# Weaving the first mixing visit into the second half of the phases, and plain products for two visits (long convolution with wave-MLP, one core)

## Chip, cores and metric

The kernel runs on one core of a Trainium2 chip. The metric is the device time of one execution in microseconds (us), lower is better. T, S and the other marks on the time axis are read from the profiled execution of each kernel and count from the start of its span.

## The reference

```python
B, S, D = 8, 5696, 128
y  = irfft(rfft(x, 2*S) * rfft(h, 2*S))[:, :S]     # long convolution, per batch and channel
theta = y @ w_theta                                 # phases
zr, zi = y * cos(theta), y * sin(theta)
m  = einsum('ts,bsd->btd', w_tok_r, zr) + einsum('ts,bsd->btd', w_tok_i, zi)   # token mixing
u  = y + m
out = u + maximum(u @ w_ch, 0)
```

The kernel first does the convolution, then the phases of the first 2816 tokens in two halves (batches 0 to 3, then 4 to 7; 22 steps of 128 tokens each), then the token mixing, which takes the rest, some 1585 of 2175 us, other work running behind it. Mixing goes in "visits" of two pairs of output tiles; its operand b (z of these tokens, eleven blocks of 128 x 4096 bf16, each with a left half from batches 0 to 3 and a right half from batches 4 to 7) stays in SBUF for a whole pass of 22 visits. Most visits are by Strassen's scheme, seven products in place of eight, for which VectorE makes sums of the parts of b; the first visit was by plain products while those sums were made.

## The kernel before, where the change touches it

```python
# last group of the convolution: y (yt) to HBM
    if then is not None:
        then(yt)                       # ya of the second phase half, SBUF to SBUF, on SyncE
    for e in range(2):
        nc.sync.dma_start(yt_hbm[...], yt[64 * e:64 * e + 64]...)
# ... cut ...
def phase_step(ti, hh):                # one of 22 steps of a half
    yT = st[hh][:, :, ti * P:(ti + 1) * P]
    # 4 transposes (tpz), 10 theta matmuls, then
    def copy():
        nc.vector.tensor_copy(y_ap, tpz)
        nc.sync.dma_start(y2_hbm[ti]..., y_ap...)
    phases_b(ti, y_ap, 4 * hh, 4, yT, ..., copy=copy)
# phases_b: three activations (ScalarE), zr and zi into zz (VectorE), then per 64 rows
    nc.sync.dma_start(z_hbm[:, p_, j, i, :, cols].rearrange("z t n -> t z n"), zz[rows])
# ... cut ...
def load_b(p, j, pool):                # a block of b back from HBM
    t_ = pool.tile([P, 7 * 1024], BF16, tag=f"b{j}", name=f"b{j}")
    for z in range(2):
        eng = nc.scalar if p or j >= NE else nc.sync
        eng.dma_start(t_[:, z * 2048:(z + 1) * 2048], z_hbm[z, p, j]...)

for step in steps0:                    # first half
    step()
for n, ti in enumerate(tile_order):    # second half, b blocks loaded behind it
    phase_step(ti, 1)
    if n % 4 == 3:
        while len(bts_of[0]) < min(n // 2, NE):
            load_b(0, len(bts_of[0]), bpe)
# ... cut: mixing ...
classic = tt == 0                      # visit 0 plain, all others Strassen
if classic:
    for n in range(4):
        for j in range(nj):
            # 4 products of 512 columns per block and n
    for j in range(nj):
        sums_apart(bts[j0 + s0 + j]); sums_in_place(bts[j0 + s0 + j])     # VectorE
    for c, z, m_ in (...):
        nc.vector.tensor_tensor(c, z, ms[m_], op=add)                     # y added by VectorE
```

## Time and profile before

2178.68 us (median of 3 runs, 2177.13 to 2178.82); the span of the profiled run is 2175.5 us. The stages, from the table of busy time in chosen windows:

| stage | from, us | to, us | TensorE busy, us | clock | DMA share |
|---|---|---|---|---|---|
| end of convolution, first phase half | 400.0 | 463.5 | 48.6 | 0.95 | 0.67 |
| second phase half | 463.5 | 549.4 | 34.6 | 0.71 | 0.98 |
| visit 0 | 549.4 | 590.8 | 41.0 | 0.94 | 0.94 |
| from visit 1 to the end | 590.8 | 2175.5 | about 15 us of waits | 1.00 (to 1286.4) | 0.93 (to 1286.4) |

Read it so: after 590.8 us TensorE is full and its clock is full, so there nothing can be gained but by less work. "Clock" is the share of TensorE's full clock that was granted, "DMA share" the mean busy share of the core's 16 DMA engines as the profile counts it, which can pass 1. Names in the profile: yt is y as the convolution leaves it; ya is y of one phase half as the steps read it, and two copies ya<-yt fill the last part of the second half's; tpz and theta_ps are a step's transposes and phases on TensorE; y_ap is the copy of y that is stored, zz the z of one step; ring is, in the changed kernel, the place in SBUF of the early weights and of block 0 of b. Two marks: **S**, the moment at which the steps of the second half can go on because ya has landed (465.8 us), and **T**, the moment at which visit 0 is done and visit 1 starts (590.8 us). The span is S + (T - S) + rest = 465.8 + 125.0 + 1584.7.

### The profile page before, as it was taken

The numbers are of one execution on the slowest core, as the hardware profiler recorded it, in microseconds if no ns is written. First come the engines' busy times: TensorE is split into PE (matmuls) and PEld (weight loads), VectorE is DVE, ScalarE is ACT, GpSimd is POOL, SyncE is SP. The second block draws the span as 40 slices with busy tenths as digits, with TensorE's granted clock in tenths as the row PEclk, the third lists the DMA queues.
The fourth block names the chain that finished last, engine by engine and source line by source line (L and its number), as shares of the span: only waits on it lengthen the run. The fifth ranks groups of instructions, "written<-read, shape, count | busy, mean of one in ns | idle before, by whom it ended". The sixth has DMA issues, their size and how long they took to land.

```text
span 2175.5 us, 41105 instructions
## 1 busy us (share of the span) xinstructions
PE 1998.2 (92%) x15545; PEld 1125.1 (52%) x15723; DVE 1619.4 (74%) x2920; ACT 670.6 (31%) x984; POOL 857.1 (39%) x1572
## 2 busy tenths in 40 slices
PE   4788898763899999999999999899999999999998
PEld 4787888652344444444444444344444444444444
DVE  7767767767778888888877667667777777776867
ACT  5877877574132333333210000001111111111111
POOL 5301010002344645445466544354545453535350
PEclk8788889987899999999999999999999999999999
DMA  7356463579988989899999869687878787879794
GB/s 146 89 125 163 128 162 118 172 185 275 236 156 175 182 169 168 167 179 176 176 169 162 138 115 291 106 133 137 148 132 152 132 151 130 152 131 153 126 158 91
DMA packets 409382, 340.38 MB, mean 156 GB/s; under 512 B 83303, under 2 KB 363751, under 8 KB 408071
## 3 DMA queue, kind: packets, MB, share of 16 engines
q0 software_dynamic: 221312, 143.00, 48.7%
q1 hardware_dynamic: 183552, 179.93, 28.5%
q10 hardware_dynamic: 4320, 14.81, 1.8%
q8 instruction: 123, 2.02, 0.4%
q14 instruction: 75, 0.61, 0.1%
HBM read 381.83 MB, written 97.93 MB: 221 GB/s over the span
## 4 chain that ended last, share of the span: by engine, by line
PE 65%; DMA 5%; DVE 4%; issue 2%; ACT 2%; POOL 1%; SPq 1%; DVEq 0%; ACTq 0%; POOLq 0%
PE m L910 59%; DMA b<-z_hbm 3%; PE m L878 2%; DMA z_hbm<-zz 2%; DVE c L917 1%; PE v L680 1%; PE utp L673 1%; PE m L914 1%; DVE wt L591 1%; PE m L833 1%; POOL wb L582 1%; PE m L831 1%; ACT mag L404 0%; ACT red L405 0%; PE theta_ps L382 0%
## 5 line engine op out<-in xcount | busy, mean ns | idle before, releaser
L582 POOL DMA_DIRECT2D wb<-in_moe_w_tok_i_dram x720 | 387.9, 547 | 679.3 <-DVE wt L591 602.6
L591 DVE STREAM_TRANSPOSE wt<-wb 128x384 f32<-128x384 f32 (+2 forms) x720 | 360.2, 524 | 117.1 <-PE m L910 71.2
L582 POOL DMA_DIRECT2D wb<-in_moe_w_tok_r_dram x720 | 386.6, 548 | 146.2 <-DVE wt L591 107.0
L910 PE MATMUL m<-b,wt 128*128 128x512 bf16 x1803 | 425.7, 381 | 7.1 <-DVE wt L591 2.4
L910 PEld LDWEIGHTS <-wt 128*128 128x128 bf16 x1848 | 181.3, 98 | 225.0 <-issue 5.7
L917 DVE TENSOR_TENSOR c<-c,m 128x512 f32<-128x512 f32 x420 | 271.0, 671 | 0.4 <-PE m L910 0.4
L675 ACT ACTIVATE uts<-utp 128x512 bf16<-128x512 bf16 (+1 forms) x90 | 53.2, 592 | 607.3 <-PE utp L673 607.3
L320 PE MATMUL ps<-r_u,u_t 128*128 128x128 f16 x1024 | 133.0, 228 | 14.9 <-DVE u_t L304 11.7
L321 PE MATMUL ps<-r_v,v_t 128*128 128x128 f16 x1024 | 131.7, 227 | 0.0
L670 ACT ACTIVATE ub<-c 128x512 bf16<-128x512 f32 (+1 forms) x90 | 56.3, 628 | 224.9 <-DVE c L846 139.7
L127 POOL DMA_DIRECT2D x<-in_x_dram x64 | 34.2, 541 | 201.3 <-PE ps L190 189.3
L320 PEld LDWEIGHTS <-u_t 128*128 128x128 f16 x1024 | 106.0, 103 | 13.6 <-DVE u_t L304 13.5
L321 PEld LDWEIGHTS <-v_t 128*128 128x128 f16 x1024 | 104.9, 103 | 5.2 <-issue 3.7
L304 DVE TENSOR_TENSOR u_t<-xs,hs 128x1024 f16<-128x1024 f16 x96 | 69.6, 725 | 41.9 <-ACT xs L302 31.5
L302 ACT ACTIVATE xs<-ps 128x1024 f16<-128x1024 f32 x96 | 95.3, 1017 | 17.6 <-DVE v_t L304 8.7
L878 PE MATMUL m<-b,wt 128*128 128x512 bf16 x344 | 79.3, 387 | 15.3 <-ACT red L405 14.5
L190 PE MATMUL ps<-f_t,x 89*128 89x180 f16 x512 | 84.5, 310 | 8.0 <-ACT xs L302 5.9
L208 PEld LDWEIGHTS <-w_t 64*128 64x128 f16 x3240 | 65.5, 106 | 38.1 <-issue 24.7
L580 POOL COPY wb<-b 128x2 bf16<-128x2 bf16 x4 | 0.5, 179 | 213.2 <-DMA z_hbm<-zz 213.2
L190 PEld LDWEIGHTS <-x 89*128 89x128 f16 x512 | 73.8, 237 | 10.1 <-issue 9.4
L384 ACT ACTIVATE red<-theta_ps,magic 128x512 f32<-128x512 f32 (+1 forms) x46 | 31.6, 687 | 140.8 <-PE theta_ps L382 107.4
L623 ACT ACTIVATE yb<-tpz 128x512 bf16<-128x512 bf16 (+1 forms) x46 | 27.4, 597 | 153.6 <-PE tpz L621 137.4
(2713 smaller groups left out, 3824.5 us busy)
## 6 DMA issues: line engine op xcount, KB each, us to landing
wb<-in_moe_w_tok_r_dram POOLq DMA_DIRECT2D x352, 96.0 KB, 4.5
wb<-in_moe_w_tok_i_dram POOLq DMA_DIRECT2D x352, 96.0 KB, 5.0
wb<-in_moe_w_tok_r_dram POOLq DMA_DIRECT2D x352, 80.0 KB, 4.2
wb<-in_moe_w_tok_i_dram POOLq DMA_DIRECT2D x352, 80.0 KB, 3.7
hs<-hf_hbm SPq DMA_DIRECT2D x192, 128.0 KB, 3.2
cp_hbm<-c SPq DMA_DIRECT2D x88, 256.0 KB, 2.3
c<-cp_hbm SPq DMA_DIRECT2D x88, 256.0 KB, 4.0
out_dram<-c SPq DMA_DIRECT2D x88, 256.0 KB, 4.2
```

Source lines behind the costliest of these rows:

```text
L190: nc.tensor.matmul(ps[:, i // 2, (i % 2) * 2 * K1:(i % 2 + 1) * 2 * K1], lhs(q + i), f1_t[:NB], start=True, stop=True)
L208: nc.tensor.matmul(ps[:, e, j * HD:(j + 1) * HD], w_t2[rows, c0 + j, N2 * (1 - ri):N2 * (3 - ri)], a_st["a"][rows, ri * K1 + c0 + j, :], s ...
L302: nc.scalar.activation(xs[:, :, :, :ck], ps, AF.Copy)
L304: nc.vector.tensor_tensor(uv[r][:, :, :, c0:c0 + ck], xs[:, :, :, :ck], hv[:, r:r + 1, :, :ck].to_broadcast([P, 2, HD, ck]), op=mult)
L320: nc.tensor.matmul(o, u_t[:, at:at + P], r_u, start=True, stop=False)
L321: nc.tensor.matmul(o, v_t[:, at:at + P], r_v, start=False, stop=True)
L582: nc.gpsimd.dma_start(wb[32 * i:32 * i + 32, :ng, :nj * 64], bass.AP(tensor=a.tensor, offset=a.offset + row0 * S + p * H + i * QR + j0 * 6 ...
L591: nc.vector.transpose(wt.rearrange("p j t r -> p (j t r)").bitcast(F32).rearrange("p (j g t) -> p g j t", j=TJ, g=4)[:, :ng, :nj], wb[:, : ...
L670: nc.scalar.activation(ub[:m].rearrange("p b d -> p (b d)"), c[:m], AF.Copy)
L878: nc.tensor.matmul(ms[n // 2 * 2 + h], a[n][:, j, :, r], bts[jj][n % 2 * 2 + h][:, r, :], start=(n % 2 == 0 and jj == 0 and r == 0), stop= ...
L910: nc.tensor.matmul(ms[q], a[q][:, j, :, r], bts[jj][q][:, r, :], start=(jj == 0 and r == 0), stop=(jj == NJ - 1 and r == 1 and q not in left))
L917: nc.vector.tensor_tensor(c, z, ms[q], op=op)
```

## The change

Its intent: TensorE idles through the second phase half, so do the products of visit 0 there, four after each step. For this, z of the right half goes from SBUF straight into b for nine of eleven blocks, left halves are fetched ahead, the weights of visits 0 and 1 are fetched before the phases end, stores of y and part of z move from SyncE to GpSimd's queue, visit 1 becomes plain too so that VectorE's sums can be spread over more time, and y is added on TensorE by identity matmuls and evacuated by ScalarE.

```diff
@@ the last yt stores, the stores of y in the second half @@
-                    nc.sync.dma_start(yt_hbm[...], yt[...])
+                    (nc.gpsimd if then else nc.sync).dma_start(yt_hbm[...], yt[...])
-            nc.sync.dma_start(y2_hbm[ti]..., y_ap...)
+            (nc.gpsimd if hh else nc.sync).dma_start(y2_hbm[ti]..., y_ap...)
@@ z straight into b @@
+            if tags is None and j in home:
+                for r in range(2):
+                    (nc.gpsimd if e and r else nc.sync).dma_start(
+                        home[j][32 * i:32 * i + 32, :4096]...[:, :, q_, r], zz[e * 64 + r:e * 64 + 64:2])
+            elif tags is None:
+                nc.sync.dma_start(z_hbm[:, p_, j, q_, i].rearrange("z t n -> t z n"), zz[rows])
@@ weights early, in a ring where a table of the convolution was @@
+    def open_ring():
+        ring["all"] = keep.tile([P, K1 * 3 * N2], BF16, tag="keep", name="ring")
+        pump()
@@ left halves ahead @@
+    def load_b_half(j):
+        t_ = home_of[j] = tile_b(0, j, home_pool(j))
+        for z in range(2):
+            nc.gpsimd.dma_start(t_[:, z * 2048:z * 2048 + 1024], z_hbm[z, 0, j, 0]...)
+    for j in range(7):
+        load_b_half(j)
     for step in steps0:
         step()
@@ the weave: blocks 0 to 5 of visit 0 in four quarters, left column half first @@
+        if i == 1:
+            for q, (h, s) in enumerate(((0, 0), (0, 1), (1, 0), (1, 1))):
+                for n in range(4):
+                    for j in range(TJ):
+                        product((held, a)[s], s * TJ + j, j, n, (h,))
+                        if (n * TJ + j) % 2:
+                            next_steps(1)
@@ blocks 9 and 10 still through HBM, once the phases are done @@
+        for j in range(len(bts_of[0]), NJ):
+            load_b(0, j, bp)
@@ plain visit 1, y by identity matmuls @@
-            classic = tt == 0
+        classic = plain(p, tt)           # tt == 0 or (p == 0 and tt == 1)
+                        if n == 1:
+                            nc.tensor.matmul(ms[m_], ident_bf, z, start=False, stop=True)
+                        else:
+                            for b in range(4):
+                                nc.tensor.matmul(ms[m_][:, b * D:(b + 1) * D], z[:, b, :], ident_bf, ...)
+                        nc.scalar.activation(c, ms[m_], AF.Copy)
... (cut: the ring of weights, the spread of VectorE's sums, the order of background work)
```

## The prediction

> **What bounds the kernel now.** I read the page's busy table and slices first, then the busy time by stage, then the waits of TensorE in two windows, then the time order of single engines around the change of stage.
>
> ```profile
> PE   4788898763899999999999999899999999999998
> PEclk8788889987899999999999999999999999999999
> ```
>
> From slice 11 (598 us) on TensorE is full at full clock: that is the token mixing. Slices 8 to 10, counted from 0 (435 to 598 us), are the hole: there the second half of the phases runs (theta, sine, cosine, z for batches 4 to 7). The stages, from the table of busy time in chosen windows (us, then busy us and count of each engine, clock, DMA share, GB/s):
>
> ```profile
> 400.00:463.50 63.50, 48.57 (x690) 41.41 (x701) 47.79 (x76) 43.95 (x76) 0.00 (x0) 0.95 0.67 172
> 463.50:549.40 85.90, 34.58 (x304) 25.00 (x309) 57.77 (x106) 43.50 (x76) 19.11 (x39) 0.71 0.98 254
> 549.40:590.80 41.40, 41.02 (x188) 18.75 (x192) 30.17 (x53) 8.01 (x13) 11.61 (x22) 0.94 0.94 230
> 590.80:1286.40 695.60, 686.95 (x3408) 323.42 (x3476) 560.00 (x1092) 171.10 (x276) 360.71 (x664) 1.00 0.93 166
> ```
>
> Row 2, the second phase half, lasts 85.9 us with TensorE busy 34.6 (and that at a clock of 0.71) and no compute engine over 58; the DMA share is 0.98. Row 3 is the first mixing visit (plain products), row 4 the Strassen visits of pass 0. Who held TensorE up, in 463 to 591 us:
>
> ```profile
> PE ps L482 <- ACT red L405: 34.6, 16, 10.2
> PE m L878 <- ACT red L405: 14.5, 1, 14.5
> ```
>
> ScalarE is named, but it was itself starved, as its time order shows (idle before, then releaser):
>
> ```profile
> 531.35 0.60 ACT L404 ACTIVATE mag<-ps 128x512 f32<-128x512 f32 x1 [9.78 <-DVE y_ap L486]
> 548.16 0.60 ACT L404 ACTIVATE mag<-ps 128x512 f32<-128x512 f32 x1 [7.21 <-DVE y_ap L486]
> ```
>
> The copy into y_ap waits for a free y_ap, that is for the store of y to HBM, which sits in SyncE's queue behind stores of z and loads of b. So the stage is bound by transfers: z goes out to HBM and comes back as b, while weights are already being loaded. Where nothing blocks (480 to 493 us) a step takes 1.66 us, ScalarE's three activations. Mixing then begins cold:
>
> ```profile
> 549.38 0.59 PE L878 MATMUL m<-b,wt 128*128 128x512 bf16 x1 [14.51 <-ACT red L405]
> 590.84 1.46 PE L910 MATMUL m<-b,wt 128*128 128x512 bf16 x6
> 595.59 2.72 PE L910 MATMUL m<-b,wt 128*128 128x512 bf16 x6 [2.21 <-DVE c L893]
> ```
>
> After 590.8 TensorE waits for some 15 us in all up to the end, so what counts is when the visit after the first begins, plus the work that is left then.
>
> **What the Trainium skill says.** "TensorE: Matmul & The Clock Gate", section "Back-to-back issue gap": N/2.4 + 2.5 ns for a warm matmul of N columns, 216 ns at 512. The trace agrees: starts at 1286.65, 1286.86, 1287.08 us. The same page, "Why this matters for your kernels", wants no TensorE gaps over some 3 us lest the clock halve; here it fell to 0.71 on average in row 2, and the first matmul after the gap has 0.59 us instead of 0.38. "DMA: Bandwidth & Descriptors", "Issuing engines are not separate DMA queues": DMAs of all issuers run on the same 16 engines, so moving stores from SyncE to GpSimd saves issue time only. Row 2's 0.98 agrees. "PSUM — Partial Sum Buffer", "Engine vs sequencer instructions": matmuls start and complete in program order. So mixing woven between phase steps cannot slip past a blocked step; the 34.6 us above show such blocking.
>
> **The change part by part.** Let T be the time at which the second mixing visit starts. Before, T = 590.8.
>
> (a) Weaving. The first six of eleven j blocks of visit 0 (6 x 16 = 96 matmuls of 512 columns) go between the 22 phase steps: 96 x 0.216 = 20.7 us. A step on TensorE has 4 transposes and 8 theta matmuls of 128 columns and 2 of 512: 2560 columns, 12 x 0.056 + 2 x 0.216 = 1.1 us; 22 of them 24 us. Sum 45 us, or 2.0 us per step with its four products, more than ScalarE's 1.66. Start: the first step of this half ran at 463.5 and waited for ya until 465.8. I take 465, so these would end at 510 if only TensorE counted. The left halves need no second-half phases, so the first two of four quarters can start at once; the scratch banks of the phases are apart from the four accumulators.
>
> (b) Five more j blocks: 80 x 0.216 = 17.3 us, then 2 identity matmuls of 512 and 8 of 128, 0.9 us. Ideal T = 510 + 18 = 528. The accumulators are evacuated by ScalarE (4 x 0.6 us beside), so the wait of 2.2 us for DVE c goes.
>
> (c) Transfers in 465 to 528. z of the right half goes SBUF to SBUF, 22 x 256 KB = 5.8 MB, written once and not read back for nine of eleven blocks. y 22 x 128 KB = 2.9 MB. Blocks 9 and 10 still come from HBM, 2.1 MB. Left halves: nine of 0.5 MB; their places (and the ring's) come free one by one from 400 us on and their z is complete tile by tile, so I guess that five load before 463, where row 1 has a share of only 0.67, and 2 MB remain. Final yt and ya 2 MB. Together 14.8 MB on the queues that took 28.5% of the 2175 us for 180 MB, 3.45 us per MB: 51 us. Six weight loads of 0.38 MB on the queue with 48.7% for 143 MB, 7.4 us per MB: 17 us. Sum 68 us of 63 us of window. In stretches of 20 us the share reached 1.04 to 1.15 between 520 and 580 us, so it almost fits, but it comes in bursts: I add 9 us. T = 537. Before, the same stage also sent 8 MB of b back in.
>
> (d) Visit 1 plain, not Strassen: 176 instead of 154 matmuls, +22 x 0.216 = 4.8 us, plus 0.9 us of identities. Two background steps move from visit 0 to later, +0.9 us.
>
> (e) Operand sums: 11 x 5 of 0.6 us (0.68 busy) = 33 us of DVE, formerly all in visit 0, now spread up to visit 2. DVE in the rest of visit 0 and in visit 1: 48 sums 29 us, some 24 transposes 12 us, background 6 us, weight sums 3 us: 50 us of 57. Close; I allow 2 us of waits.
>
> (f) Removed after T: the wait and cold clock around 593 us, -3 us.
>
> Rest: before 2175.5 - 590.8 = 1584.7 us; after 1584.7 + 4.8 + 0.9 + 0.9 + 2 - 3 = 1590.3. Span 537 + 1590 = 2127; the times lie 2 to 3 us above the span (2178.7 to 2175.5): 2130 us, 2.2% less.
>
> **The rivals.** First, the weave flows: transfers and issue hide entirely, T = 528 and no DVE waits: 2119 us. For it: TensorE needs 2.0 us per step where ScalarE needs 1.66, and z no longer makes the round trip. Against it: the 68 us of transfers above. Second, the queues become the bound. GpSimd must issue per step a y store and part of z (about 1.0 us, from its 0.547 us per issue), plus 24 weight pieces and left halves (15 to 20 us): 37 to 42 us of 45, in order. One late landing there holds up the stores of y, four y_ap run out, and in-order TensorE stops the products too. SyncE has three z pieces per step; its z stores take 0.59 us to issue, 1.8 us per step at worst. If steps took 2.6 us, T = 550: 2143 us. Third, the early weights (2.4 MB from about 400 us, 17 us of DMA) delay ya for the first phase half, whose loads are issued at 400.5 and 404 us; a late ya stops TensorE in order. At most 5 us, partly absorbed since TensorE is busy only 48.6 of 63.5 us in row 1. Fourth, DVE becomes the bound in visit 1 (85% or more even by my count): +5 to 10 us. Fifth, the gain is hidden anyway: unlikely, since TensorE has no slack after 600 us, so an earlier start comes out nearly whole at the end.
>
> **Range and chances.** The limit for over 2% is 2135 us, 5 us above my sum. The queues and DVE could cost 10 to 15 us more, a smooth weave gives back 11. So 2112 to 2150 for 8 in 10; faster by over 2% 0.65, within 2% 0.33, slower 0.02.
>
> **What would show it.** Right: TensorE over 85% busy from 470 us on, with the clock near 1; the last phase step at about 515 us; the second visit starting at 528 to 546; z landing in b directly; the later visits at 33.5 us each as now. Wrong: TensorE waiting on ScalarE or VectorE during the weave with gaps of 5 us and more (queues or DMA, second rival); waits for ya before 430 us (third); TensorE waiting for wt or b sums in visits 1 and 2 (fourth); a start at 537 with an end that has not moved by as much, which would mean a new loss in the steady visits.

## The result, and the profile after

The changed kernel takes 2153.16 us (median of 4 runs, 2152.45 to 2157.64) against 2177.96 us (2177.13 to 2178.82) of the kernel before in the same rounds: a ratio of 0.989, with a 95% interval of 0.9873 to 0.9908. A ratio is the mean time of one kernel's runs over that of the other's runs of the same rounds, so it is not quite the ratio of the medians quoted. The result is correct. It is 1.1% faster, and 3 us above the predicted range of 2112 to 2150. The profiled run is the slowest of the four (span 2155.9 us), which matters for a few us below.

The two rows of the page that the prediction began with, busy tenths of TensorE and granted clock in 40 slices of 54 us, now of the changed kernel:

```profile
PE   3788889768999999999999997999999999999998
PEclk8699879999999999999999999999999999999999
```

The hole in slices 8 to 10, counted from 0 (6, 3, 8 before), has become 6, 8, 9, with the clock at 9 in place of 8, 7, 8: largely filled, but not its first third. The same stages as before, of the changed kernel (from:to and length in us, then busy us and count of TensorE, weight load, VectorE, ScalarE, GpSimd, then clock, DMA share, GB/s):

```profile
400.00:463.50 63.50, 48.12 (x732) 41.58 (x742) 51.18 (x83) 47.43 (x81) 15.21 (x28) 0.95 0.95 228
463.50:549.40 85.90, 63.42 (x448) 37.01 (x457) 53.52 (x100) 43.08 (x74) 46.12 (x84) 0.87 0.92 240
549.40:590.80 41.40, 40.11 (x184) 18.03 (x186) 26.78 (x48) 9.64 (x16) 13.97 (x27) 0.89 0.76 152
590.80:1286.40 695.60, 687.37 (x3409) 324.70 (x3477) 554.95 (x1084) 172.69 (x279) 357.45 (x658) 1.00 0.92 165
```

In the second row TensorE is busy 63.4 us where it was 34.6, in the time that half of the phases took before, but the DMA share is still 0.92: the weave runs in a stage that transfers fill. The first row's DMA share has gone from 0.67 to 0.95. The last row is as before. The same stretch cut where the changed kernel changes its pace:

```profile
470.85:490.00 19.15, 12.38 (x80) 7.74 (x83) 10.75 (x21) 9.83 (x17) 11.32 (x21) 0.77 1.01 341
490.00:520.00 30.00, 29.07 (x253) 18.21 (x256) 22.00 (x40) 22.57 (x40) 22.82 (x42) 1.00 0.98 230
520.00:533.40 13.40, 10.06 (x60) 5.61 (x60) 6.29 (x13) 7.91 (x14) 4.39 (x8) 0.75 0.74 189
533.40:562.40 29.00, 23.34 (x100) 10.03 (x100) 18.93 (x36) 1.82 (x4) 13.93 (x26) 0.82 0.87 188
562.40:602.20 39.80, 39.59 (x202) 18.88 (x205) 30.04 (x53) 12.81 (x22) 13.00 (x25) 1.00 0.81 153
```

Row 2 is the weave as it was meant: TensorE busy 29.07 of 30 us at full clock. Before it (row 1) and after it (row 3) it stalls at a reduced clock, and the tail of visit 0 (row 4) is slow too. Row 5 is the plain visit 1, full. S and T by TensorE's time order (start, length, then idle before and its releaser):

```profile
470.85 0.29 PE L561 MATMUL tpz<-ident_bf,ya 128*128 128x128 bf16 x1 [5.42 <-DMA ya<-yt]
561.84 0.61 PE L1002 MATMUL m<-ident_bf,yy 128*128 128x128 bf16 x8
```

S = 470.85 and T = 561.84 + 0.61 = 562.45 us. The rest after T is 2155.9 - 562.45 = 1593.5 us. The prediction had S = 465, T = 537 and a rest of 1590.3. So of the 29 us by which this profiled span passes the predicted 2127, 25 lie before T: 6 us in S and 20 us in T - S (91.6 in place of 72); the other 3 are in the rest. What TensorE waited for from 463 to 620 us (us in all, times, longest; the first four of seven lines):

```profile
PE tpz L561 <- DMA ya<-yt: 6.9, 2, 5.4
PE m L964 <- DMA b<-z_hbm: 5.8, 4, 3.4
PE tpz L561 <- DVE y_ap L569: 5.2, 2, 3.7
PE m L964 <- DMA b<-zz: 3.9, 2, 3.2
```

Before, 49 us of such waits stood against ScalarE and, behind it, the stores of y; now four kinds of waits share what is left, three for transfers and one for y_ap. A wait costs more than its own length, since matmuls after it run at the lower clock: in row 1 the waits and the clock of 0.77 took 19.15 us for 80 matmuls. GpSimd's queue in the same time (start, length, issues, idle before):

```profile
457.85 1.11 POOL L354 DMA_DIRECT2D yt_hbm<-yt  x2 [22.11 <-issue]
471.69 4.26 POOL L626 DMA_DIRECT2D b<-z_hbm  x8 [12.74 <-DMA z_hbm<-zz]
...
485.44 0.54 POOL L570 DMA_DIRECT2D y_hbm<-y_ap  x1
```

Only block 0's left half was loaded before S; the eight others go out from 471.69 us on, and the first store of y of this half stands behind them until 485.44. VectorE, too, was held up in this stretch:

```profile
479.50 0.69 DVE L417 TENSOR_TENSOR zz<-red,y_ap 128x512 bf16<-128x512 f32 x1 [4.63 <-DMA z_hbm<-zz]
```

It waited 4.63 us here, and 2.74 us more at 483.87, until stores of the first half's last z had landed and their zz was free. And the two ya copies, from issue to landing, before and after:

```profile
ya<-yt SPq DMA_DIRECT2D x2, 352.0 KB, 4.1
```
```profile
ya<-yt SPq DMA_DIRECT2D x2, 352.0 KB, 9.2
```

### The profile page after: what moved, and what is told of

It is laid out like the page before. It is cut to its first block, busy times and chain, and to the rows that moved or that the text cites. A ratio compares the mean times of both kernels' runs of the same rounds, so it can differ in the third digit from the quotient of the medians.

```text
span 2155.9 us, 41270 instructions
## 1 busy us (share of the span) xinstructions
PE 2000.3 (93%) x15586; PEld 1124.8 (52%) x15765; DVE 1599.6 (74%) x2884; ACT 674.7 (31%) x992; POOL 889.7 (41%) x1628
## 4 chain that ended last, share of the span: by engine, by line
PE 64%; DVE 3%; DMA 2%; issue 1%; ACT 0%; POOL 0%; DVEq 0%; ACTq 0%
PE m L1034 58%; PE m L964 2%; DMA b<-z_hbm 2%; DVE c L1041 1%; PE v L776 1%; PE utp L769 1%; PE m L1038 1%; DVE wt L689 1%; PE m L921 1%; PE m L919 1%; PE theta_ps L385 0%; PE tpz L717 0%; DMA yT<-yt_hbm 0%; DMA y_hbm<-ring 0%; POOL ring L493 0%
## 5 line engine op out<-in xcount | busy, mean ns | idle before, releaser
L493 POOL DMA_DIRECT2D ring<-in_moe_w_tok_i_dram x720 | 388.2, 547 | 686.2 <-DVE wt L689 612.1
L493 POOL DMA_DIRECT2D ring<-in_moe_w_tok_r_dram x720 | 386.8, 548 | 240.9 <-PE ps L211 103.5
L689 DVE STREAM_TRANSPOSE wt<-ring 128x384 f32<-128x384 f32 (+2 forms) x720 | 357.9, 522 | 116.3 <-PE m L1034 69.9
L1034 PEld LDWEIGHTS <-wt 128*128 128x128 bf16 x1804 | 176.6, 98 | 215.7 <-DVE wt L689 3.2
L1041 DVE TENSOR_TENSOR c<-c,m 128x512 f32<-128x512 f32 x412 | 265.1, 669 | 0.4 <-PE m L1034 0.4
L771 ACT ACTIVATE ring<-utp 128x512 bf16<-128x512 bf16 (+1 forms) x86 | 50.9, 592 | 608.6 <-PE utp L769 608.6
L307 DVE TENSOR_TENSOR u_t<-xs,hs 128x1024 f16<-128x1024 f16 x96 | 69.8, 727 | 42.8 <-ACT xs L305 23.8
L964 PEld LDWEIGHTS <-wt 128*128 128x128 bf16 x528 | 51.4, 101 | 69.8 <-issue 17.0
L719 ACT ACTIVATE ring<-tpz 128x512 bf16<-128x512 bf16 (+1 forms) x46 | 27.4, 597 | 137.2 <-PE tpz L717 115.8
```

The lines of the kernel that those rows point to most:

```text
L307: nc.vector.tensor_tensor(uv[r][:, :, :, c0:c0 + ck], xs[:, :, :, :ck], hv[:, r:r + 1, :, :ck].to_broadcast([P, 2, HD, ck]), op=mult)
L493: nc.gpsimd.dma_start(wb[32 * i:32 * i + 32, :ng, :nj * 64], bass.AP(tensor=a.tensor, offset=a.offset + row0 * S + p * H + i * QR + j0 * 6 ...
L689: nc.vector.transpose(wt.rearrange("p j t r -> p (j t r)").bitcast(F32).rearrange("p (j g t) -> p g j t", j=TJ, g=4)[:, :ng, :nj], wb[:, : ...
L964: nc.tensor.matmul(ms[n // 2 * 2 + h], a[n][:, j, :, r], bts_of[p][jj][n % 2 * 2 + h][:, r, :], start=(n % 2 == 0 and jj == 0 and r == 0), ...
L1034: nc.tensor.matmul(ms[q], a[q][:, j, :, r], bts[jj][q][:, r, :], start=(jj == 0 and r == 0), stop=(jj == NJ - 1 and r == 1 and q not in left))
L1041: nc.vector.tensor_tensor(c, z, ms[q], op=op)
```

## The experiments

The question was which of these made the 25 us between the predicted and the measured T. Theories at the start: A, separate losses (a late ya, left halves that wait for their place, the tail of blocks 9 and 10, SyncE's many issues), each worth its waits; B, the stage is bound by the 16 DMA engines, so that taking one wait away brings up another. A third question arose, what the weave itself had brought. Kernels were made, on five chips, each with runs of the kernel before on its own chip. All numbers in one table ("full DMA" is DMA share times T - S, that is, how long all 16 engines would need if their packets took the same time; it falls by itself when the stage gets shorter, so it is a description and no proof of a bound):

| run | median us (range) | ratio to before | S | T | T - S | rest | full DMA |
|---|---|---|---|---|---|---|---|
| before | 2178.0 (2177.1 to 2178.8) | 1 | 465.8 | 590.8 | 125.0 | 1584.7 | 121 |
| change | 2153.2 (2152.5 to 2157.6) | 0.9890 | 470.9 | 562.4 | 91.6 | 1593.5 | 84 |
| e11_after_again | 2152.3 (2146.3 to 2157.1) | 0.9881 | 471.8 | 560.3 | 88.5 | 1589.3 | 84 |
| e1_yt_sync | 2151.1 (2149.2 to 2155.0) | 0.9883 | 468.5 | 561.9 | 93.4 | 1591.3 | 90 |
| e2_places | 2148.6 (2144.6 to 2152.7) | 0.9869 | 469.3 | 553.0 | 83.7 | 1589.8 | 79 |
| e3_half_issue (wrong) | 2152.1 (2147.2 to 2153.0) | 0.9878 | 468.4 | 557.1 | 88.7 | 1594.1 | 89 |
| e4_no_tail (wrong) | 2147.5 (2147.2 to 2151.5) | 0.9868 | 470.9 | 553.8 | 82.9 | 1591.9 | 79 |
| e5_three (wrong) | 2143.0 (2140.3 to 2145.3) | 0.9841 | 471.9 | 546.9 | 75.1 | 1591.6 | 77 |
| e6_pe_order | 2158.4 (2155.4 to 2159.4) | 0.9908 | 472.8 | 562.2 | 89.4 | 1595.1 | 84 |
| e7_unwoven | 2162.7 (2160.3 to 2165.5) | 0.9932 | 474.1 | 565.7 | 91.6 | 1594.0 | 83 |
| e8_strassen1 | 2162.1 (2160.7 to 2171.4) | 0.9938 | 469.3 | 557.7 | 88.4 | 1602.5 | 82 |
| e9_places_act | 2147.7 (2144.9 to 2152.2) | 0.9863 | 470.4 | 550.5 | 80.1 | 1592.6 | 78 |
| e10_places_sync | 2153.7 (2151.5 to 2156.7) | 0.9889 | 467.8 | 559.8 | 92.1 | 1592.6 | 89 |
| e12_four (wrong) | 2140.4 (2135.8 to 2144.9) | 0.9824 | 473.9 | 548.6 | 74.7 | 1594.4 | 75 |
| e13_by_need | 2154.5 (2148.5 to 2160.4) | 0.9894 | 470.8 | 559.6 | 88.8 | 1592.3 | 86 |
| e14_need_places | 2148.0 (2145.8 to 2152.3) | 0.9866 | 470.8 | 552.0 | 81.2 | 1592.1 | 78 |
| e15_need_unwoven | 2158.4 (2152.4 to 2160.4) | 0.9906 | 476.1 | 563.4 | 87.3 | 1595.2 | 79 |
| e16_no_left (wrong) | 2144.3 (2142.2 to 2146.0) | 0.9849 | 469.5 | 550.5 | 81.0 | 1589.9 | 79 |
| e17_no_left_tail (wrong) | 2147.6 (2144.9 to 2151.8) | 0.9866 | 470.4 | 552.5 | 82.1 | 1591.9 | 79 |
| e18_no_left_tail_issue (wrong) | 2136.2 (2133.5 to 2138.4) | 0.9809 | 469.6 | 539.4 | 69.8 | 1592.0 | 68 |

A single kernel's four runs scatter by 4 to 12 us and the 95% intervals of the ratios are about 0.0025 either way (5 us), so differences of 3 us of time prove nothing; T - S comes from one trace each, and the two traces of the change differ by 3 us. "Wrong" kernels give a wrong result.

**e1_yt_sync**: the last store of yt back on SyncE.

```diff
-                    (nc.gpsimd if then else nc.sync).dma_start(yt_hbm[...], yt[...])
+                    nc.sync.dma_start(yt_hbm[...], yt[...])
```

> Undoes one part: the last store of yt goes back to SyncE's queue, behind the copies ya<-yt, instead of GpSimd's queue, ahead of them. In the changed kernel these copies landed 9.2 us after issue (4.1 before), and the first step of the second phase half went on at 470.9 us instead of the 465 that I had assumed. Theory A (the store takes the transfer engines from the copies): copies land in 4 to 5 us, that step goes on at 465 to 466 us, visit 1 starts 3 to 6 us earlier (now 563 us), the time falls to 2147 to 2151 us. Theory B (the weave is bound by the queues that issue, so a late start is caught up, or SyncE now carries the store as well): visit 1 starts within 2 us of 563, the time is 2151 to 2156 us.

Measured: the ya copies land in 3.6 us (9.2 in the change), so it was the yt store ahead that slowed them. The ya wait before S falls to 0.3 us; S is only 2.4 us earlier, since the second copy was issued 3 us later in this trace (464.65 against 461.58 us). T is 561.9 as in the change, because T - S grows to 93.4; the left halves now go out at 476 to 490 us, even later. A wait taken away came back elsewhere.

**e2_places**: the places of blocks 1 to 6 in reverse order, so that block 1 does not lie where yt of the convolution still waits to be stored.

```diff
+    early = {j: bpe[0].tile([P, BT], BF16, tag=f"b{j}", name=f"b{j}") for j in range(6, 0, -1)}
     def tile_b(p, j, pool):
-        t_ = ring["all"][:, WB:WB + BT] if j == 0 else pool.tile(...)
+        t_ = (ring["all"][:, WB:WB + BT] if j == 0 else early[j] if p == 0 and j in early else pool.tile(...))
```

> Same arithmetic; only the places of b1 to b6 in their pool are reversed, so that b1 no longer lies where g and yt of the last convolution group lay. In the changed kernel the load of b1's left half waited in GpSimd's queue until 471.7 us and all other left halves and the y stores stood behind it. Theory A (it waited for its place): the loads of b1 to b4 issue right behind the yt store at 458 to 462 us, the y stores of the steps start some 8 us earlier than 485 us, the waits of TensorE for y_ap (5.2 us) and b<-z_hbm in the weave (1.3 us) shrink, visit 1 starts 4 to 8 us earlier, 2145 to 2149 us. Theory B (the transfer engines are full there anyway, share 0.97 to 1.02 from 460 to 520 us, so the bytes only move): within 2 us of the changed kernel, 2151 to 2156 us.

Measured: correct, 2148.6 us; T - S falls by 5 to 8 us against the change's two traces. Six left-half loads now go out ahead of S, in GpSimd's time order, but TensorE's time order shows what they do to ya:

```profile
453.58 3.22 POOL L629 DMA_DIRECT2D b<-z_hbm  x6
```
```profile
469.30 0.29 PE L561 MATMUL tpz<-ident_bf,ya 128*128 128x128 bf16 x1 [10.47 <-DMA ya<-yt]
```

The wait for ya is 10.5 us where it was 5.4. The second ya copy was issued 5.4 us earlier than in the change (456.14 against 461.58) but landed only 1.5 us earlier, for it took 13.1 us where it took 9.2: the loads that came forward shared the DMA engines with it. Part of the gain was given back at once.

**e3_half_issue** (wrong, relative error 0.30): one copy of 64 partitions into b in place of two of 32, same bytes, half the issues, all of them on SyncE; GpSimd, which issued one in four, has none left.

```diff
-                for r in range(2):
-                    (nc.gpsimd if e and r else nc.sync).dma_start(home[j][32 * i:32 * i + 32, :4096]..., zz[e * 64 + r:e * 64 + 64:2])
+                nc.sync.dma_start(home[j][64 * (i // 2):64 * (i // 2) + 64, :4096]..., zz[rows])
```

> Wrong result on purpose: each step writes its z into b with two copies of 64 partitions instead of four of 32, same bytes, all on SyncE, into the wrong rows. Theory A (issue bounds the weave: SyncE issued 38 of these back to back in 27.7 us, 0.73 us each, three per step): SyncE's queue has gaps, the last z copy is issued at 525 to 530 us instead of 539, TensorE's wait of 3.2 us for b<-zz goes, visit 1 starts 8 to 14 us earlier, 2140 to 2146 us. Theory B (the bytes bound it): no change of more than 3 us, 2150 to 2156 us.

The suspicion came from SyncE's time order in the change:

```profile
495.33 27.67 SPq L431 DMA_DIRECT2D b<-zz  x38
```

38 issues back to back, 0.73 us each, three per step: 2.2 us of issuing for a step of 1.95 us, so SyncE falls behind. Measured: the waits for z in b are gone, but y_ap waits rise to 9.9 us, the DMA share of the stage is 1.00, and T - S (88.7) and the time (2152.1) are those of the change within the noise. Alone, the issues are not the bound.

**e4_no_tail** (wrong, relative error 0.048): visit 0 takes blocks 7 and 8 in place of 9 and 10, which come from HBM after the phases.

```diff
-                                     bts_of[p][jj][n % 2 * 2 + h][:, r, :],
+                                     bts_of[p][jj if p or tt else min(jj, 8)][n % 2 * 2 + h][:, r, :],
```

> Wrong result on purpose: visit 0 uses blocks 7 and 8 in place of 9 and 10, which come late through HBM; they are then needed only at the end of visit 1. Theory A (the last two blocks' way through HBM holds up the end of visit 0: waits of 4.5 us and a cold clock, 8.8 us lost between 545.6 and 562.3 us): visit 1 starts at 553 to 556 us, 2143 to 2147 us. Theory B (the wait only takes the place of another, such as DVE's transposes and sums that stand at the same spot): less than 3 us gained, 2150 us or more.

Measured: T - S 82.9, 6 to 9 us less, and 2147.5 us. The tail is real; the prediction had 17.3 + 0.9 us for the blocks after the last step and no wait for their loads.

**e5_three** (wrong): e2, e3 and e4 together.

> Wrong on purpose (the joint of places, half issue and no tail): the places of six left halves reversed, z into b by one copy of 64 partitions where there were two of 32, and blocks 9 and 10 of visit 0 replaced by blocks 7 and 8. Alone they moved the start T of the second visit from 562.3 us to 552.8, 556.9 and 553.8 in their profiles, and the time from 2153 us by -4.6, -1.0 and -5.7 us. Theory A (three separate losses, which add): T = 562.3 - 9.5 - 5.4 - 8.5 = 539 us, which is within 2 us of the predicted 537, and 2126 to 2134 us. Theory B (they hide one another: when one goes, the next wait takes its place): T of 546 to 554 us, 2138 to 2146 us.

Measured: T - S 75.1, which is near the sum of the parts (91.6 - 7.9 - 2.9 - 8.7 = 72.1), but the ya wait is again 10.8 us and T only 546.9; the time, 2143.0 us, is that of theory B. So inside T - S the causes nearly add, and S takes some of it back.

**e6_pe_order** and **e7_unwoven**: TensorE held in program order through visits 0 and 1 (a control), and the same with all 22 steps ahead of the products, the weave alone undone.

```diff
-            ordered.enter_context(tc.manual_schedule(engines={DVE}))
+            ordered.enter_context(tc.manual_schedule(engines={DVE} if p else {DVE, PE}))
```
```diff
-                next_steps(2)
+                next_steps(22)
```

> Control for the next run, correct result: TensorE is kept in the program's order too through the first two visits, as VectorE is already, so that the products stand exactly four after each step. Both theories: T within 4 us of 562, 2149 to 2157 us. If the scheduler's own order was part of the loss, T is 552 or less and the time 2144 or less.

> Correct result, TensorE in program order as in the control, but all 22 steps of the second phase half first and the products of visit 0 after them: the weave alone undone, everything else of the change kept (z straight into b, left halves ahead, plain visit 1, identity matmuls). Theory A (the weave is what gained: TensorE idles through the phases again): the steps end no earlier than in the change, about 521 us, since the y stores and the z copies set their pace, then 176 products of 0.216 us and the identities, 39 us, and a cold start: T = 521 + 39 + 3 = 563 if pace is all, and 570 to 580 if the products in between did save their 21 us; 2160 to 2170 us. Theory B (the weave gained little, since the steps alone take 1.7 us instead of 2.0 and z straight into b was the gain): steps end at 512 to 516, T of 553 to 558 and 2145 to 2152 us.

Measured: the control has the T expected, its time is 1.4 us above what was expected. Without the weave T is 3.5 us later than in the control and the time 4.3 us longer. That is all that the weave brings here (both kernels hold TensorE in program order, which by the control cost some 5 us of time, not of T). The stages of e7 (steps, then products) and its main wait:

```profile
474.10:524.50 50.40, 31.87 (x287) 23.20 (x293) 34.71 (x66) 35.69 (x63) 28.65 (x52) 0.80 0.86 263
524.50:565.70 41.20, 40.02 (x197) 18.71 (x201) 23.26 (x43) 5.01 (x10) 22.29 (x42) 1.00 0.96 198
```
```profile
PE tpz L561 <- DVE y_ap L569: 18.1, 15, 4.8
```

Alone, the steps take 50.4 us (2.3 us each, held by stores of y) where the kernel before took 83.6 (465.8 to 549.4). Woven, in the control, the last step begins at 530.38, here at 524.45: the products between cost the steps 6 us, and the tail's wait comes back, since unwoven the loads of blocks 9 and 10 are hidden behind nine other blocks. So of the 28 us by which T moved (590.8 to 562.4), 25 came with the weave undone (590.8 to 565.7), from the rest of the change. What the traces show of that rest is fewer bytes: from S to T the queues moved 30.6 MB before (245 GB/s x 125.0 us) and 21.4 MB in the change (234 x 91.6 us), and the full DMA time fell from 121 to 84 us, about as much as T - S. Which part of the change made how much of it was not taken apart; z straight into b, in place of a store and a load, is the largest by bytes.

**e8_strassen1**: visit 1 by Strassen again.

```diff
-        return tt == 0 or (p == 0 and tt == 1)
+        return tt == 0
```
(with the order of background work and the place of the sums adapted)

> Correct result: visit 1 by Strassen again, as in the kernel before, with all operand sums of VectorE done by then; visit 0 and the weave as in the change. Theory A (plain visit 1 pays, for it lets 55 sums of 0.6 us, 33 us, be spread): T unchanged at 562, visit 1 has 5.7 us less of TensorE work but waits 10 to 20 us for VectorE: 2157 to 2168 us. Theory B (VectorE had the room: idle for a third of the phase stage): the 5.7 us come out, 2146 to 2149 us.

Measured: T is 557.7, 3 to 5 us earlier, but the rest is 1602.5 us, 9 to 13 longer, and the time 2162.1. ScalarE's time order in visit 1, and TensorE's waits from 557 to 605 us:

```profile
572.51 0.63 ACT L407 ACTIVATE mag<-red 128x512 f32<-128x512 f32 x1 [13.93 <-DVE red L389]
```
```profile
PE theta_ps L385 <- ACT ring L719: 6.9, 2, 3.4
```

ScalarE waited 13.9 us for VectorE, and TensorE for ScalarE; TensorE was busy 31.1 of 39.3 us. VectorE, with all 55 sums to make, is the last name in the chain, but it was itself busy only 30.4 of these 39.3 us and waited 5.9 us for a weight, so that its order and what it waits for count, not its load alone. What is shown is that the plain visit 1 pays for its 5.7 us of extra products, by some 9 us of time; by which wait exactly was not settled.

**e9_places_act**, **e10_places_sync**, **e11_after_again**: two tries to get ya through earlier on top of e2, and the change itself once more.

```diff
-                    (nc.gpsimd if then else nc.sync).dma_start(yt_hbm[...], yt[...])
+                    (nc.scalar if then else nc.sync).dma_start(yt_hbm[...], yt[...])
```
```diff
-            nc.gpsimd.dma_start(t_[:, z * 2048:z * 2048 + 1024], ...)
+            (nc.sync if 0 < j < 7 else nc.gpsimd).dma_start(t_[:, z * 2048:z * 2048 + 1024], ...)
```

> Correct result: the reversed places of six left halves as before, and the last store of yt on ScalarE's queue, so that the left halves on GpSimd's queue stand behind nothing and the ya copies on SyncE's. In the run with reversed places alone TensorE waited 10.8 us for the ya copies, which shared the DMA engines with that store and with twelve left-half loads. Theory A (the store ahead on GpSimd was part of it: left halves now go out before ya and are done by then): the ya wait falls to 5 us or less, T is 545 to 549 us, 2139 to 2145 us. Theory B (the bytes in flight count, whichever queue issues them): the ya wait stays at 8 to 11 us, T at 551 to 554, 2145 to 2150 us.

> Correct result: the reversed places, and the left halves of blocks 1 to 6 issued by SyncE, where they stand behind the two ya copies, instead of GpSimd. Theory A (ya lost its place among the DMA engines to the left halves): the ya wait falls to 5 us or less, the weave starts at 464 to 466 us, T is 545 to 550 us, 2138 to 2146 us. Theory B (SyncE has no room for twelve more issues of 0.6 us, so that the last z stores of the first half and the first z copies come 7 us later): VectorE waits for zz, T is 552 to 558 us, 2146 to 2152 us.

> The changed kernel itself once more, unaltered, so that the others of this call can be held against it on the same chip: 2150 to 2156 us, T within 4 us of 562, and a ya wait of 5 to 8 us. If it comes out at 2147 or less, the gains of 4 to 6 us read from single-part kernels are within the noise between calls.

Measured: e9 halves the ya wait (4.6 us in all), but not because ya came sooner: its copies took 11.8 us to land (9.2 in the change, 9.7 in e2), and TensorE reached them later, as the first half's own steps ended later. S stays at 470.4; T - S is 80.1 and the time 2147.7 us, within the noise of e2's. e10 loses e2's gain: T - S 92.1, the ya wait 6.7 us. SyncE had no room. The change repeated as expected. Over all variants S lies between 467.8 and 476.1 and never near 465, and in every trace it is the end of a wait for the second ya copy: the time at which that copy is issued, plus what it takes to arrive. It takes 9 us where the yt store goes ahead on GpSimd's queue, 13 where left-half loads go ahead as well (e2, e5), 11 to 12 where loads go ahead on GpSimd's and that store on ScalarE's queue (e9, e12, e14, e15), and 4 where the store goes behind (e1, and the kernel before). It is issued anywhere between 456.1 (e2) and 464.6 us (e1, e7), and between 459.3 (e3) and 462.7 (e11) in kernels whose edits touch nothing before S, so a few us of S are chance of single traces. What else sets the time of issue was not settled (in 400 to 463 us the DMA share is 0.89 to 0.96 in all variants, 0.67 before).

**e12_four** (wrong): e5 with e9's move of yt.

> Wrong on purpose (half issue and no tail take z and blocks that are not the right ones): all four losses taken away at once, that is reversed places, the last yt store on ScalarE's queue, z into b by one copy of 64 partitions where there were two of 32, and blocks 7 and 8 for 9 and 10 in visit 0. With the first two alone T was 550.5 us; without the yt move the other three gave 546.9, with 10.8 us of waits for ya, 6 more than with it. Theory A (the ideal of the prediction was right and what is above it is these four losses): T = 550.5 - 8.5 for the tail - 3 to 5 for the issue = 537 to 539 us, or 546.9 - 6 = 541; 2130 to 2137 us. Theory B (a loss that none of the four touches holds T, such as the y stores that begin at 482 us in every variant): T stays at 544 to 547 us, 2140 to 2144 us.

Measured: T - S 74.7, as e5; T is 548.6, for S came at 473.9. By T this is theory B's value. Something held the first steps that none of the four touches.

**e13_by_need**, **e14_need_places**, **e15_need_unwoven**: GpSimd's queue reordered, so that stores of y do not stand behind all the left halves; the same with e9; and that with the weave undone (TensorE in program order).

```diff
+        if j < 3:
+            fetch()
+        else:
+            late.append(fetch)        # blocks 3 to 5 after the 4th step, 6 to 8 after the 12th
```

> Correct result: the changed kernel with only the order of GpSimd's queue altered. Left halves of blocks 0 to 2 stay ahead, those of 3 to 5 are written in the program after the fourth step of the half and those of 6 to 8 after the twelfth, so that the stores of y no longer stand behind all sixteen loads. In the change the first y store went out at 485.4 us and the stage from the ya copies' landing (S) to the start of the second visit (T) took 91.6 and 88.5 us in two profiles. Theory A (the block at the head of that queue made the stall at 472 to 490 us): first y store by 476 us, no y_ap wait over 2 us before 490, T - S of 80 to 84 us, 2143 to 2148 us. Theory B (the DMA engines are full there, so that order changes nothing): T - S of 87 us or more, 2150 to 2155 us.

> Correct result: order by need, reversed places and the last yt store on ScalarE's queue together. Theory A: T - S falls from the 80.1 us of places and yt alone to 75 to 77 us, what is left being the tail of blocks 9 and 10 (some 8 us) above the 63 of the ideal and a cold start; 2140 to 2145 us, the fastest correct kernel. Theory B (the y stores wait for DMA bandwidth, not for their turn): T - S stays at 79 us or more, 2146 to 2149 us.

> Correct result: the kernel of order by need, places and yt, with the weave undone as before (all steps first, then the products, TensorE in program order). In the change itself undoing the weave cost only 3.5 us of T and 4 us of time, because the steps were held by stores of y (18.1 us of waits) either way. Theory A (the weave is worth its 21 us of hidden products once nothing blocks): T - S at least 10 us longer than with the weave, time 8 to 14 us longer. Theory B (steps alone need only ScalarE's 1.66 us, and unwoven the two blocks from HBM are hidden behind the products): T - S of 76 to 82 us, time within 5 us of the woven one.

Measured: e13 is theory B's: 2154.5 us, T - S 88.8. GpSimd's time order in e13:

```profile
473.96 0.55 POOL L570 DMA_DIRECT2D y_hbm<-y_ap  x1 [0.22 <-issue]
474.50 0.54 POOL L629 DMA_DIRECT2D b<-z_hbm  x1
480.76 0.56 POOL L431 DMA_DIRECT2D b<-zz  x1 [5.72 <-DVE zz L418]
481.31 0.57 POOL L570 DMA_DIRECT2D y_hbm<-y_ap  x1
```

The first store of y went out 11.5 us earlier than in the change, and yet the second only at 481.31, behind a copy of z that waited 5.72 us for VectorE's zz, and VectorE waited in its turn 4.30 us for a store of the first half's z to land. So taking most left halves out of the stores' way was not enough; a queue on which the stores of y stand behind nothing at all was not tried in this kernel. e14 did no better than e9 (81.2 against 80.1; in e14 the first store of y again went only at 481 us, so it is no clean test of the order). e15 is 6 us longer in T - S and 10 us in time than e14, of which the control e6 puts some 5 us down to TensorE's fixed order: the weave's worth stays about 5 us, not clearly more once places are mended.

**e16_no_left**, **e17_no_left_tail**, **e18_no_left_tail_issue** (all wrong): the left halves of blocks 1 to 8 set to zero by GpSimd, at the same point of its queue and in the same places, in place of 4 MB of loads; then with no tail; then with half the issues too.

```diff
+            if j:
+                nc.gpsimd.memset(t_[:, z * 2048:z * 2048 + 1024].bitcast(F32), 0.0)
+                continue
             nc.gpsimd.dma_start(t_[:, z * 2048:z * 2048 + 1024], ...)
```

> Wrong on purpose: the left halves of blocks 1 to 8 are not loaded (16 DMAs, 4 MB) but set to zero by GpSimd, in the same places and at the same point of its queue as in the change, so that only the bytes go and the order stays. Theory A (the DMA engines are full from 470 to 490 us: y stores, z stores and z copies land late because 4 MB of left halves share the 16 engines): at 3.45 us per MB that is 13.8 us of all engines; T - S falls from 88.5 to 91.6 us to 76 to 81 us, 2139 to 2145 us, and the DMA share of 470 to 490 us falls below 0.9. Theory B (the order of GpSimd's queue, whose head waits for its place, makes the stall): T - S stays at 86 us or more, 2149 to 2155 us.

> Wrong on purpose: no left halves and no tail (blocks 7 and 8 for 9 and 10 in visit 0) together. Theory A: the tail's 8 to 9 us come off once more, T - S of 68 to 72 us, 2132 to 2138 us. Theory B: T - S of 78 to 83 us, as no tail alone gave (82.9), 2144 to 2149 us.

> Wrong on purpose: no left halves, no tail, and z into b by one copy of 64 partitions where there were two of 32. Theory A (bytes, tail and issue are the whole of it): T - S of 63 to 68 us, where the prediction's ideal is 63, 2127 to 2134 us. Theory B (something else holds the steps): T - S of 72 us or more, 2138 us or more.

Measured, e16's first stretch from S, and e18's whole stage in three stretches:

```profile
469.49:490.00 20.51, 19.74 (x160) 12.67 (x164) 18.12 (x35) 17.06 (x30) 17.46 (x34) 0.87 0.85 205
```
```profile
469.61:490.00 20.39, 18.31 (x151) 11.91 (x155) 17.17 (x34) 15.96 (x28) 15.47 (x31) 0.91 0.91 211
490.00:520.00 30.00, 27.99 (x241) 17.11 (x243) 23.48 (x44) 24.51 (x42) 12.38 (x23) 1.00 1.01 243
520.00:539.37 19.37, 19.27 (x95) 9.02 (x96) 14.72 (x29) 1.27 (x3) 9.17 (x17) 1.00 1.02 237
```

Without the left halves' bytes the stall is gone: 160 matmuls in 20.5 us where the change did 80 in 19.15, DMA share 0.85 where it was 1.01. VectorE's waits after S for the first half's stores of z, 4.6 and 2.7 us in the change, are 0.2 and 0.4 us here: with 4 MB less on the engines these stores no longer hold it up. With e13 this says bytes rather than order, though not wholly: the memsets also passed the queue sooner (first store of y at 477.3 us in place of 485.4). e16 came out as theory A had it, at the upper edge in T - S. e17 did not: its tail's gain was taken by a new wait,

```profile
PE m L1002 <- DMA yy<-y_hbm: 9.4, 1, 9.4
```

for the load of the addend y, which was issued at 529.45 us on SyncE's queue and took 15.8 us to land; the last store of y had gone out at 523.66. Why it took so long was not settled. With half the issues too (e18) that wait is gone and all three together give T - S = 69.8 and T = 539.4, 2136.2 us: between the two expected bands, 7 us above the ideal of 63 and 2 us below the predicted 72. As in e3, the edit also takes GpSimd's share of the z copies off its queue, so the number of issues and the order of that queue change together, and which of the two lets the wait go is open. The table's last column fits a stage bound by transfers, which lasts about as long as the 16 DMA engines are busy (84 of 91.6 us in the change, 75 of 74.7 in e12, 68 of 69.8 in e18). By itself that proves nothing: in the kernel before, from 640 to 660 us, the DMA share is 1.21 and TensorE is busy 19.89 of 20 us. Nor do bytes alone set the time: e17 moved 18.1 MB in 82.1 us, e12 18.8 MB in 74.7. What is shown is what the removals gave: 7 to 11 us for the left halves' bytes (e16), 6 to 9 for the tail (e4), and 19 to 22 for these two and the halved issue together (e18).

## Why the prediction was wrong, point by point

- **(a) Weaving, its start and its pace.** The pace of 2.0 us per step is right where nothing blocks (1.95 us; TensorE busy 29.07 of 30 us). The start at 465 was wrong: 470.9 and 471.8 us. The third rival (a late ya) was laid to the early weights and the first phase half; it struck the second, whose ya took 9.2 us in place of 4.1 to land, behind the yt store that the change moved ahead of it (e1).
- **(b) Five further blocks.** The products are as counted; that the last two blocks arrive only after the phases was known from the diff, but no wait was put down for it: 6 to 9 us (e4).
- **(c) Transfers: the step that failed.** "68 us of 63 us of window", for 17.1 MB, and "I add 9 us" should have been 84 us for 21.4 MB, and 26 to 29 us over the ideal of 63. The price was right on average: 68 us for 17.1 MB is 4.0 us per MB, 84 for 21.4 is 3.9. The bytes were counted too low, even though the last yt and ya, 2 MB of the count, fell before S. The assumption that five left halves load before 463 was false: only block 0's did, so 4.2 MB in place of 2 fell into the stage, at the very moment when the first steps' y and the first half's last z went out (1.01 of DMA share at 341 GB/s from 470.85 to 490 us). Ten weight loads (3.5 MB) were issued from S to T, not six (2.3), and some 3.7 MB had not been counted at all: the first half's last y and z, the addends, the inputs of background steps and visit 0's output. And the 9 us had no term for what late transfers do in this stage: they hold zz and y_ap, which stops the steps (80 matmuls in the first 19.15 us), and they bring the last two blocks late.
- **(d), (e), (f) After T.** 1590.3 us predicted, 1593.5 and 1589.3 measured. The 3 us added from span to time set a median against another run's span; a run's own time lies 1.8 us above its span (2177.26 and 2175.5 before), a slip of 1 us. The plain visit 1 pays (e8), with VectorE last in the chain of waits when it is taken away.
- **The premise behind (a)**, that idle TensorE time is the gain to be had: e7 and its control show the weave to be worth 4 us. Unwoven, the ideal would be 22 x 1.66 us for the steps and 176 x 0.216 + 0.9 us for the products, 75.4 us in all, against 63 woven, an estimate from the prediction's own figures; with 84 us of DMA in the stage neither was reached. That this is why the difference does not come out is argued: no unwoven kernel was run with bytes, tail and issue taken away. The first row of evidence, DMA share 0.98 in the hole, said this already; the prediction read it and then counted too few transfers.
- **Rivals.** The first, a smooth weave, did not occur. The second (queues become the bound, T = 550, 2143 us) was nearest, but the queue's order and issue alone gave nothing (e13, e3); bytes, tail and issue together did (e18). The fourth (VectorE binds visit 1) did not occur, nor did the fifth (an earlier start is lost again by the end): the rest after T is as predicted.
- **Open:** what sets the issue of the second ya copy, and so a part of S; how the 19 to 22 us of e18 divide between bytes, issue and the order of GpSimd's queue; which part of the change other than the weave made most of its 25 us; whether e2, e9 and e14 (2147.7 to 2148.6 us, correct) are truly faster than the change, as their three like medians suggest though each interval overlaps its own: 4 to 5 us, none a proof.

## What to carry to other kernels

Before putting work into an engine's idle time, ask what makes it idle. Where it waits for transfers and the DMA share is near 1 (the share alone says little: it was 1.21 beside a full TensorE), list every transfer of that stage, with those left over from the stage before and those fetched for the next, price them in DMA time, and take bytes out first; the weave comes after. Test a suspected wait both by its order and by its bytes, since taking one wait away here brought up another in five of the kernels (e1, e2, e3, e5, e17). What is to go out early must also have its place free early: loads meant to be ahead were late, and those brought forward, like a store put first (e1), delayed a more urgent copy.

## What the Trainium skill lacked or had wrong

- "DMA: Bandwidth & Descriptors", section "Issuing engines are not separate DMA queues", calls the issue time "usually small relative to the DMA itself". For one copy that holds here: 0.73 us to issue 64 KB on SyncE, against a median of 4.2 us from issue to landing. For a queue it was not small: three copies per step are 2.2 us of issuing for a step of 1.95 us, 38 back to back. Halving the count gave nothing alone (e3); in e18, where GpSimd's queue changed with it, it took e17's 82.1 us to 69.8.
- No page read says by how much a transfer put ahead delays a small urgent copy: ya's two copies of 352 KB took 9.2 us to land with 1.4 MB of yt ahead of them, 3.6 with it behind (e1), and the second took 13.1 with six left-half loads ahead as well (e2).
- No page read gives a rate for mixed traffic of small SBUF-to-SBUF copies and stores: 230 GB/s at a DMA share of 0.98 here, against 341 GB/s at 1.01 with 256 KB loads in it.
